# Moving the sums and low parts of one fp32 network kernel from GpSimd to VectorE, each placed apart

## The chip, the cores and the metric

One core of one Trainium2 chip runs the whole program. The metric is the device time of one execution in microseconds (us), lower is better. Engines are named as in the profile: PE is TensorE (matrix products), PEld its weight load, DVE is VectorE, ACT is ScalarE, POOL is GpSimd, SP is SyncE, whose queue issues the DMAs.

## The reference

A channel attention over 6016 tokens and 256 channels, followed by two feed-forward networks with 2048 hidden channels, all in fp32:

```python
qn = q / (np.linalg.norm(q, axis=1, keepdims=True) + 1e-06)
kn = k / (np.linalg.norm(k, axis=1, keepdims=True) + 1e-06)
s = kn.transpose(0, 2, 1) @ qn / tau
a = softmax(s)                       # rows of a 256 x 256 matrix
x = v @ a                            # 6016 x 256
h = x @ moe_w_in
x = (h * np.clip(h + 3.0, 0.0, 6.0) / 6.0) @ moe_w_out
r = np.maximum(x @ moe2_w_in, 0.0)
return (r * r) @ moe2_w_out
```

## The kernel before

**Arithmetic.** Every fp32 operand of a product is kept as two tiles of a rounded type (fp32r): a high part, which ScalarE makes by a cast, and a low part, the value less its high part, which is one subtraction. `passes` then issues three matmuls for one product (lines 308, 309 and 310: high by high, low by high, high by low). The attention matrix is multiplied into the first network's input weights, so the kernel computes two feed-forward networks one after the other (`j` = 0 and 1).

**Tiling.** The tokens lie in six pairs of blocks (`p` = 0 to 5), each block 512 tokens wide and 448 in the last pair. The hidden channels lie in eight units (`u`) of 256. For each pair and unit `strassen` multiplies a 2 x 2 block of weights by a 2 x 2 block of tokens with seven products in place of eight; the pair (0, 0) alone goes the plain way. One unit is 21 matmuls for the seven products and 24 that multiply the activated hidden values by the output weights (`group`): 45 matmuls. There are eleven Strassen pairs, so 88 units.

**What the seven products need.** For tokens: the sums T1 to T4 of the four blocks, and seven high and seven low parts, made by `prepare` for the next pair while the current one runs (`combination`: line 708, low parts: line 715; 11 subtractions a pair). For weights: four sums (`combine`, line 214) and their low parts, made by `m1_sum` and `m1_sums_split` for the first network's four blocks `c4`, and by `second_in` (sums, line 214; `rests`, line 244) and `second_out` (line 123) for each of eight parts of the second network, which are written to DRAM and read back when the second network begins. All of these subtractions and sums run on GpSimd: 16 instructions of `m1_sum`, 8 of `m1_sums_split`, 121 of `prepare`, 48 of `second_in` and 8 of `second_out`, 201 in all. The raw weights come as float64 and are turned into fp32 by two ScalarE and four VectorE instructions (`from_float64`, lines 152 to 165).

**What VectorE does in a unit.** Eleven instructions of the unit's width: three sums that finish a hidden block (line 761; one operand comes from PSUM), four activations (line 775 in the first network, 780 in the second; where the hidden block is `h` both operands lie in SBUF, where it is `y` one lies in PSUM) and four low parts of the activated blocks (line 123, `gs<-g,gs`, both operands in SBUF).

**The order.** It is written out by hand: `at(place, go)` puts a step at a place, and `run` issues the steps of all engines by rising place. A unit is 15 places (`SLOTS`), one place for each group of three matmuls, and a unit's steps have fixed places after its start (`PLACE`, `chain`, `GROUP`). Each engine then runs its own steps in that order, as early as its operands allow. The place numbers below count from the first Strassen unit; the eight units of pair p of the first network begin at 120 (p - 1), those of the second at 600 + 120 p. GpSimd's steps go through `on_pool`, which moves a step later by 0.3 until it stands at least `POOL_APART` = 3.2 places from every other step so placed.

Of the kernel before, what the change touches and what calls it, by code (L numbers as in the profile page):

```python
# [41 lines left out]
POOL_APART = 3.2  # L42
# [11 lines left out]
def attention_then_two_ffns(  # L54
# [63 lines left out]
    def split(hi, lo, x, part=2, rest=None):  # L118

        if part != 1:  # L120
            nc.scalar.copy(hi, x)  # L121
        if part != 0:
            (rest or nc.vector).tensor_tensor(out=lo, in0=x, in1=f32(hi), op=ALU.subtract)  # L123
# [83 lines left out]
    def combine(i, st, a, b):  # L207
# [6 lines left out]
        nc.gpsimd.tensor_tensor(out=b(st, to), in0=x, in1=y, op=op)  # L214

    def second_in(u):
# [25 lines left out]
        def rests(i):  # L242
            a, w = ((slice(0, S1), x[:, :S1, :]), (slice(S1, None), st))[i]
            nc.gpsimd.tensor_tensor(out=lo[:, a, :], in0=w, in1=f32(hi[:, a, :]), op=ALU.subtract)
# [7 lines left out]
    def second_out(u):  # L252
# [6 lines left out]
        def parts(x, part):  # L259
# [3 lines left out]
            split(t[:, 0, :], t[:, 1, :], x, part, rest=nc.gpsimd)  # L263
# [48 lines left out]
    with tc.manual_schedule():  # L312
# [166 lines left out]
        def m1_keep(c4):  # L479
            for k in range(KC):  # L480
                if k == 0:
                    m32[c4] = spare(2 * c4 + 1, f"m32_{c4}").rearrange("p (k f) -> p k f", k=KC)
# [195 lines left out]
        def prepare(j, p, start, end):  # L678
# [15 lines left out]
            def combination(r):  # L694
# [13 lines left out]
                nc.gpsimd.tensor_tensor(out=to, in0=x, in1=y, op=ALU.subtract)  # L708
# [10 lines left out]
            for i, r in enumerate((T1, T2)):  # L719
                on_pool(start + 12 + 4 * i, lambda r=r: combination(r))  # L720
            for r, x in when.items():
                at(start + x, lambda r=r: hi(r))
                on_pool(start + x + 1.7, lambda r=r: lo(r))
            for i, r in enumerate((T3, T4)):
                on_pool(start + 32 + 4 * i, lambda r=r: combination(r))

            first_pair = {T3: 0.3, T1: -14.5, B22: 4.3, T4: -10.5}
            for i, r in enumerate((T3, T1, B22, T4)):
                after = first_pair[r] if (j, p) == (0, 1) else end - SLOTS + 8.3 + 4 * i
                at(after, lambda r=r: hi(r))  # L730
                on_pool(after + 1.7, lambda r=r: lo(r))
# [222 lines left out]
```

## Time and profile before

| | us |
|---|---|
| runs of before | 1064.50, 1062.21, 1064.21; median 1064.21 |
| profiled execution, whole | 1063.71 |
| its span, first to last instruction | 1061.9 |
| TensorE busy | 1042.6 |
| VectorE busy | 864.2 |
| ScalarE busy | 664.6 |
| GpSimd busy | 251.4 |

Busy times are the time in which an engine had an instruction under way. Matmuls overlap each other, so that TensorE can count as busy and still run below its pace: what tells its pace is how many matmuls it starts in a stretch of time. A row of the timeline gives the start, the duration, the engine, the source line, the operation and its tiles; in square brackets it gives how long the engine stood idle before and what ended that.

### The profile page before, as it was taken

To read this page: it belongs to the slowest core of one execution; us is meant where nothing else is said; L and a number is where in the kernel's file an instruction comes from. 1 tells how busy PE (TensorE), PEld (TensorE's weight loads), DVE (VectorE), ACT (ScalarE), POOL (GpSimd) and SP (SyncE) were. 2 spreads that over 40 slices of the span, in tenths; PEclk is the share of its full clock that TensorE was granted. 3 is DMA by queue.
4 is the path that set the end of the run, shared out by engine and by line. 5 is a ranking of instruction groups with operands and counts; after the bars stand their busy time and mean duration, and the time that the engine had idled before them with its cause. 6 is when DMAs were issued, how large, how long until landed. Compare 5 with 4: busy or idle time off the path is not lost.

```text
span 1061.9 us, 13045 instructions
## 1 busy us (share of the span) xinstructions
PE 1042.6 (98%) x4630; PEld 865.0 (81%) x4630; DVE 864.2 (81%) x1283; ACT 664.6 (63%) x1200; POOL 251.4 (24%) x211
## 2 busy tenths in 40 slices
PE   9999999999999999999999999999999999999998
PEld 8867777887877888787998888888888888888997
DVE  7898867898898889888889678678778878778766
ACT  6777767777777778776777445455445445545443
POOL 0012244343134133324233022113103104103000
PEclk9999999999999999999999999999999999999999
DMA  9911203102302301320765100100200200200100
GB/s 352 349 42 40 80 1 120 55 20 95 119 0 102 137 31 40 115 90 0 243 236 211 49 1 36 44 1 6 74 1 1 80 1 0 75 1 1 40 1 35
DMA packets 25938, 77.65 MB, mean 73 GB/s; under 512 B 2833, under 2 KB 4881, under 8 KB 25873
## 3 DMA queue, kind: packets, MB, share of 16 engines
q1 hardware_dynamic: 25872, 76.82, 20.4%
q8 instruction: 36, 0.59, 0.2%
q14 instruction: 30, 0.24, 0.1%
HBM read 52.95 MB, written 23.86 MB: 72 GB/s over the span
## 4 chain that ended last, share of the span: by engine, by line
PE 78%; DVE 14%; ACT 6%; issue 2%; POOL 0%; ACTq 0%; POOLq 0%
PE acc L310 13%; PE acc L308 13%; PE acc L309 13%; PE y L308 6%; PE y L309 6%; PE y L310 6%; DVE gs L123 4%; PE s L298 4%; PE q L308 3%; PE q L309 3%; PE q L310 3%; DVE g L775 3%; PE x L308 2%; PE x L310 2%; PE x L309 2%
## 5 line engine op out<-in xcount | busy, mean ns | idle before, releaser
L123 DVE TENSOR_TENSOR gs<-g,gs 128x512 fp32r<-128x512 f32 (+1 forms) x384 | 293.2, 764 | 71.3 <-ACT gs L784 61.7
L310 PE MATMUL acc<-gs,wo 128*128 128x512 f32 (+1 forms) x768 | 298.2, 388 | 5.1 <-DVE gs L123 5.0
L308 PE MATMUL acc<-gs,wo 128*128 128x512 f32 (+1 forms) x768 | 296.6, 386 | 1.6 <-ACT gs L121 1.0
L309 PE MATMUL acc<-gs,wo 128*128 128x512 f32 (+1 forms) x768 | 296.0, 385 | 0.0
L784 ACT CAST gs<-g 128x512 fp32r<-128x512 f32 (+1 forms) x352 | 208.5, 614 | 79.5 <-DVE g L775 55.9
L310 PEld LDWEIGHTS acc<-gs,wo 128*128 128x128 f32 x768 | 144.1, 188 | 39.9 <-DVE gs L123 12.9
L308 PEld LDWEIGHTS acc<-gs,wo 128*128 128x128 f32 x768 | 144.3, 188 | 29.9 <-ACT gs L121 2.2
L309 PEld LDWEIGHTS acc<-gs,wo 128*128 128x128 f32 x768 | 144.3, 188 | 26.7
L715 POOL TENSOR_TENSOR x<-raw,x 128x512 fp32r<-128x512 f32 (+1 forms) x55 | 73.1, 1330 | 368.6 <-ACT x L711 367.1
L780 DVE SCALAR_TENSOR_TENSOR g<-h 128x512 f32<-128x512 f32 (+1 forms) x144 | 120.5, 837 | 0.0
L761 DVE TENSOR_TENSOR h<-q,se 128x512 f32<-128x512 f32 (+1 forms) x88 | 59.5, 676 | 64.3 <-ACT se L757 64.3
L757 ACT COPY se<-y 128x512 f32<-128x512 f32 (+1 forms) x88 | 50.6, 575 | 92.5 <-PE y L310 92.2
L775 DVE SCALAR_TENSOR_TENSOR g<-r,h 128x512 f32<-128x512 f32 (+1 forms) x120 | 104.5, 871 | 3.5 <-ACT r L767 2.9
L757 ACT COPY su<-y 128x512 f32<-128x512 f32 (+1 forms) x88 | 50.8, 577 | 87.4 <-PE y L310 77.1
L767 ACT ACTIVATE r<-h,three 128x512 f32<-128x512 f32 (+1 forms) x120 | 85.6, 714 | 12.5 <-DVE h L761 12.2
L769 ACT ACTIVATE r<-y 128x512 f32<-128x512 f32 (+1 forms) x48 | 28.3, 590 | 56.7 <-PE y L310 56.6
L761 DVE TENSOR_TENSOR h<-q,su 128x512 f32<-128x512 f32 (+1 forms) x88 | 59.2, 673 | 1.0
L761 DVE TENSOR_TENSOR h<-x,sa 128x512 f32<-128x512 f32 (+1 forms) x88 | 59.1, 672 | 0.0
L757 ACT COPY sa<-y 128x512 f32<-128x512 f32 (+1 forms) x88 | 50.7, 576 | 7.0 <-PE y L310 0.9
L780 DVE SCALAR_TENSOR_TENSOR g<-y,r 128x512 f32<-128x512 f32 (+1 forms) x48 | 32.5, 677 | 19.9 <-ACT r L769 19.6
L298 PE MATMUL s<-qk 128*128 128x256 f32 x188 | 42.8, 389 | 0.0
L298 PEld LDWEIGHTS s<-qk 128*128 128x128 f32 x188 | 36.4, 196 | 5.5 <-DMA qk<-in_qk 0.6
(234 smaller groups left out, 1856.8 us busy)
## 6 DMA issues: line engine op xcount, KB each, us to landing
qk<-in_qk SPq DMA_DIRECT2D x23, 512.0 KB, 7.4
wo<-in_w_out SPq DMA_DIRECT2D x16, 512.0 KB, 5.8
wi<-in_w_in SPq DMA_DIRECT2D x10, 512.0 KB, 4.9
x2d<-o SPq DMA_DIRECT2D x20, 256.0 KB, 2.6
raw<-x2d SPq DMA_DIRECT2D x10, 512.0 KB, 5.8
out<-o SPq DMA_DIRECT2D x20, 256.0 KB, 2.3
raw<-in_vt SPq DMA_DIRECT2D x8, 512.0 KB, 6.4
wo2d<-wo2s SPq DMA_DIRECT2D x8, 512.0 KB, 3.0
```

Source lines behind the costliest of these rows:

```text
L123: (rest or nc.vector).tensor_tensor(out=lo, in0=x, in1=f32(hi), op=ALU.subtract)
L298: nc.tensor.matmul(s_ps[i], lhsT=x[:, C + i * P:C + (i + 1) * P], rhs=x[:, :C], start=(t == 0), stop=(t == NT - 1))
L308: nc.tensor.matmul(ps, lhsT=ah, rhs=bh, start=first, stop=False, skip_group_check=more)
L309: nc.tensor.matmul(ps, lhsT=al, rhs=bh, start=False, stop=False, skip_group_check=more)
L310: nc.tensor.matmul(ps, lhsT=ah, rhs=bl, start=False, stop=last, skip_group_check=more)
L715: nc.gpsimd.tensor_tensor(out=l, in0=ts[r], in1=f32(h), op=ALU.subtract)
L757: nc.scalar.copy(s[tag], s["y"])
L761: nc.vector.tensor_tensor(out=s[which], in0=s[ps], in1=s[tag], op=ALU.add)
L767: nc.scalar.activation(s["r" + which], h, AF.Relu, bias=three)
L775: nc.vector.scalar_tensor_tensor(out=g, in0=s["r" + which], scalar=6.0, in1=h, op0=ALU.min, op1=ALU.mult)
L780: nc.vector.scalar_tensor_tensor(out=g, in0=h, scalar=0.0, in1=r, op0=ALU.max, op1=ALU.mult)
L784: nc.scalar.copy(gs[which][0], s["g" + which])
```

## The change

From the second Strassen pair on, all of GpSimd's sums and low parts are issued on VectorE. GpSimd keeps those of the pair (0, 1), 11 instructions, and of the weight blocks c4 = 0 and 1, 12 instructions; the other 178 move. `on_pool` becomes `extra`: every step that goes through it now stands at least `APART` = 2.6 places from every other (3.2, as before, for places up to 0). The VectorE steps of `from_float64` for the second network's weights go through `extra` too, one by one (`converted`), where before they stood at fixed places. The sums of the weight blocks c4 = 2 and 3 begin at places 10 and 34 (before -9 and 17), and the second network's weights are prepared from unit 3.5 on, one part each 4.05 units (before from unit 2, each 4.5).

```diff
-POOL_APART = 3.2
+APART = 2.6
+APART_FIRST = 3.2
...
-    def combine(i, st, a, b):
+    def combine(i, st, a, b, eng=nc.vector):
...
-        nc.gpsimd.tensor_tensor(out=b(st, to), in0=x, in1=y, op=op)
+        eng.tensor_tensor(out=b(st, to), in0=x, in1=y, op=op)
...
-            nc.gpsimd.tensor_tensor(out=lo[:, a, :], in0=w, in1=f32(hi[:, a, :]), op=ALU.subtract)
+            nc.vector.tensor_tensor(out=lo[:, a, :], in0=w, in1=f32(hi[:, a, :]), op=ALU.subtract)
...
-            split(t[:, 0, :], t[:, 1, :], x, part, rest=nc.gpsimd)
+            split(t[:, 0, :], t[:, 1, :], x, part)
...
+        def idle_first(first):
+
+            return nc.gpsimd if first else nc.vector
...
-            split(hi, lo, m1_st[c4][:, u, :, :], part, rest=nc.gpsimd)
+            split(hi, lo, m1_st[c4][:, u, :, :], part, idle_first(c4 < 2))
...
-        def on_pool(place, go):
-
-            while any(abs(place - x) < POOL_APART for x in taken):
+        def extra(place, go):
+
+
+            while any(abs(place - x) < (APART if place > 0 else APART_FIRST) for x in taken):
                 place += 0.3
             taken.append(place)
             at(place, go)
...
-                nc.gpsimd.tensor_tensor(out=to, in0=x, in1=y, op=ALU.subtract)
+                idle_first((j, p) == (0, 1)).tensor_tensor(out=to, in0=x, in1=y, op=ALU.subtract)
...
-                nc.gpsimd.tensor_tensor(out=l, in0=ts[r], in1=f32(h), op=ALU.subtract)
+                idle_first((j, p) == (0, 1)).tensor_tensor(out=l, in0=ts[r], in1=f32(h), op=ALU.subtract)
...
-        for c4, x in enumerate((-100, -72, -9, 17)):
+        for c4, x in ((0, -100), (1, -72), (2, 10), (3, 34)):
             for i in range(4):
-                x = on_pool(x, lambda c4=c4, i=i: m1_sum(c4, i)) + 1
+                x = extra(x, lambda c4=c4, i=i: m1_sum(c4, i)) + 1
             for u in range(2):
-                at(x + 3 + u, lambda c4=c4, u=u: m1_sums_split(c4, u, 0))
+                at(x + 2 + u, lambda c4=c4, u=u: m1_sums_split(c4, u, 0))
             for u in range(2):
-                x = on_pool(x + 5 - 4 * u, lambda c4=c4, u=u: m1_sums_split(c4, u, 1))
+                x = extra(x + 4 - 3 * u, lambda c4=c4, u=u: m1_sums_split(c4, u, 1))
...
+        def converted(begin, make):
+
+            made = []
+            at(begin, lambda: made.extend(make()))
+            at(begin + 8.7, lambda: made[0][0]())
+            x = begin + 8.7
+            for i in range(1, 4):
+                x = extra(x + (1.6, 1.6, 1.3)[i - 1], lambda i=i: made[0][i]())
+            return made, x
+
         def prepare_in(u, begin):
-            made = []
-            at(begin, lambda: made.extend(second_in(u)))
-            for i, x in enumerate((8.7, 9.5, 17.3, 19.4, 22.4)):
-                at(begin + x, lambda i=i: made[0][i]())
-            x = begin + 22.4
+            made, x = converted(begin, lambda: second_in(u))
+            at(x + 1.6, lambda: made[0][4]())
+            x += 4
             for i in range(4):
-                x = on_pool(x + 3, lambda i=i: made[1](i))
-            at(x + 4, lambda: made[2]())
+                x = extra(x, lambda i=i: made[1](i)) + 0.7
+            at(x + 1, lambda: made[2]())
+            x += 3.5
             for i in range(2):
-                x = on_pool(x + 6 - 2 * i, lambda i=i: made[3](i))
-            at(x + 6, lambda: made[4]())
+                x = extra(x, lambda i=i: made[3](i))
+            at(x + 4, lambda: made[4]())
...
         for u in range(NU):
-            prepare_in(u, (2 + 4.5 * u) * SLOTS)
-            prepare_out(u, (4.25 + 4.5 * u) * SLOTS)
+            prepare_in(u, (3.5 + 4.05 * u) * SLOTS)
+            prepare_out(u, (5.5 + 4.05 * u) * SLOTS)
```

`prepare_out` is rewritten in the same way with `converted` and `extra`. The line numbers of the changed file are higher by one near `combine` and by ten in `prepare` and `strassen`.

What this makes of VectorE's order is seen at the start of pair (0, 3). `g`, `h` and `gs` are a unit's activated blocks, hidden blocks and their parts, `o` an output block that leaves PSUM, `tawi`/`tawo` the conversion of the second network's weights, `wa2s` the low parts of its weights, `x` and `raw` the tokens of the next pair, and the two numbers after a name are pair and unit. Before:

```order
L775 SCALAR_TENSOR_TENSOR g_3_0_3173<-r_3_0_3164,h_3_0_3137 128x512
L160 SCALAR_TENSOR_TENSOR tawi_3_3109<-tbwi_3_3110,tawi_3_3109 128x512
L581 TENSOR_SCALAR o_2_1_0_3179<-acc_2_1_0_2446 128x512
L165 ISA tawi_3_3109<-tawi_3_3109,tywi_3_3111 128x1024
L761 TENSOR_TENSOR h_3_0_3197<-q_3_0_3159,se_3_0_3186 128x512
L123 TENSOR_TENSOR gs_3_0_3192<-g_3_0_3173,gs_3_0_3192 128x512
L581 TENSOR_SCALAR o_2_0_1_3211<-acc_2_0_1_2428 128x512
L775 SCALAR_TENSOR_TENSOR g_3_0_3222<-r_3_0_3206,h_3_0_3197 128x512
L775 SCALAR_TENSOR_TENSOR g_3_0_3233<-r_3_0_3224,y_3_0_3098 128x512
L761 TENSOR_TENSOR h_3_0_3239<-q_3_0_3159,su_3_0_3155 128x512
```

The same stretch of VectorE's order now:

```order
L725 TENSOR_TENSOR x_3_6_3141<-raw_3_1_2750,x_3_6_3141 128x512
L124 TENSOR_TENSOR gs_2_7_3150<-g_2_7_3143,gs_2_7_3150 128x512
L785 SCALAR_TENSOR_TENSOR g_3_0_3166<-r_3_0_3157,h_3_0_3130 128x512
L245 TENSOR_TENSOR wa2s_3034<-w_2_2771,wa2s_3033 128x384
L590 TENSOR_SCALAR o_2_1_0_3172<-acc_2_1_0_2423 128x512
L245 TENSOR_TENSOR wa2s_3034<-w_2_2771,wa2s_3033 128x512
L771 TENSOR_TENSOR h_3_0_3189<-q_3_0_3152,se_3_0_3178 128x512
L124 TENSOR_TENSOR gs_3_0_3183<-g_3_0_3166,gs_3_0_3183 128x512
L590 TENSOR_SCALAR o_2_0_1_3203<-acc_2_0_1_2411 128x512
L785 SCALAR_TENSOR_TENSOR g_3_0_3210<-r_3_0_3198,h_3_0_3189 128x512
L161 SCALAR_TENSOR_TENSOR tawo_2_2915<-tbwo_2_2916,tawo_2_2915 128x512
L785 SCALAR_TENSOR_TENSOR g_3_0_3224<-r_3_0_3213,y_3_0_3094 128x512
```

The low parts of the pair's own tokens and of the second network's weights now stand between the unit's steps, and the two conversion steps (lines 160 and 165) ahead of `h` have gone to other places.

GpSimd's order at the same place of the program, before:

```order
L715 TENSOR_TENSOR x_3_3_3058<-raw_3_0_2753,x_3_3_3058 128x512
L715 TENSOR_TENSOR x_3_4_3084<-t_3_0_2830,x_3_4_3084 128x512
L715 TENSOR_TENSOR x_3_5_3115<-raw_3_1_2754,x_3_5_3115 128x512
L715 TENSOR_TENSOR x_3_6_3148<-raw_3_1_2754,x_3_6_3148 128x512
L244 TENSOR_TENSOR wa2s_3065<-w_2_2750,wa2s_3064 128x384
L244 TENSOR_TENSOR wa2s_3065<-w_2_2750,wa2s_3064 128x512
L123 TENSOR_TENSOR wo2s_2975<-tawo_2_2877,wo2s_2975 128x512
L214 TENSOR_TENSOR w_3_3215<-w_3_3215 128x128 x4
```

GpSimd's order now ends with the pair (0, 1), the one that the first Strassen units multiply:

```order
L718 TENSOR_TENSOR raw_1_1_1169<-raw_1_1_1169,t_1_1_1248 128x512
L725 TENSOR_TENSOR x_1_4_1436<-t_1_0_1247,x_1_4_1436 128x512
L725 TENSOR_TENSOR x_1_6_1459<-raw_1_1_1169,x_1_6_1459 128x512
L725 TENSOR_TENSOR x_1_3_1497<-raw_1_0_1168,x_1_3_1497 128x512
L725 TENSOR_TENSOR x_1_5_1516<-raw_1_1_1169,x_1_5_1516 128x512
L962 UNCONDITIONAL_BRANCH
```

Nothing of pair (0, 3) or of the second network's weights is left on GpSimd.

## Rows read from the trace of the kernel before

**Rows 1.** The page's head and busy times: us, share of the span, instructions.
```profile
span 1061.9 us, 13045 instructions
...
PE 1042.6 (98%) x4630; PEld 865.0 (81%) x4630; DVE 864.2 (81%) x1283; ACT 664.6 (63%) x1200; POOL 251.4 (24%) x211
```
**Rows 2.** Busy by stretch: pairs (0,2) to (0,5), (1,1), six units of (1,5).
```profile
core 0: us, PE busy (x) PEld busy (x) DVE busy (x) ACT busy (x) POOL busy (x), PEclk, DMA share, GB/s
...
237.82:324.14 86.32, 82.91 (x361) 67.12 (x360) 74.29 (x106) 64.26 (x114) 25.08 (x23) 1.00 0.19 66
324.14:410.34 86.20, 83.57 (x361) 68.38 (x360) 74.97 (x106) 63.49 (x113) 28.04 (x24) 0.98 0.23 83
410.34:494.96 84.62, 83.49 (x361) 67.05 (x360) 72.36 (x103) 62.99 (x114) 28.48 (x26) 1.00 0.22 77
494.96:570.56 75.60, 74.84 (x361) 67.08 (x360) 67.75 (x103) 57.58 (x111) 27.11 (x24) 1.00 0.56 195
651.60:733.24 81.64, 81.64 (x362) 67.58 (x361) 63.31 (x91) 40.66 (x73) 15.61 (x12) 1.00 0.09 26
...
987.96:1042.68 54.72, 54.72 (x272) 50.72 (x271) 38.12 (x68) 24.19 (x48) 0.00 (x0) 1.00 0.04 16
```
**Rows 3.** Waits of TensorE: us in total, times, longest us.
```profile
PE acc L310 <- DVE gs L123: 5.0, 8, 1.8
PE q L308 <- DVE h L761: 3.6, 2, 2.6
```
**Rows 4.** Timeline of VectorE ahead of TensorE's longest wait: start, us.
```profile
329.69 1.77 DVE L775 SCALAR_TENSOR_TENSOR g<-r,h 128x512 f32<-128x512 f32 x1
...
332.81 1.77 DVE L775 SCALAR_TENSOR_TENSOR g<-r,h 128x512 f32<-128x512 f32 x1
334.51 1.77 DVE L160 SCALAR_TENSOR_TENSOR tawi<-tbwi,tawi 128x512 int32<-128x512 int32 x1
...
336.80 0.67 DVE L165 CUSTOM_DVE_ANT_0 tawi<-tawi,tywi 128x1024 uint16<-128x1024 uint16 x1
337.40 0.68 DVE L761 TENSOR_TENSOR h<-q,se 128x512 f32<-128x512 f32 x1
```
**Rows 5.** Timeline of GpSimd in the same stretch.
```profile
330.88 3.16 POOL L244 TENSOR_TENSOR wa2s<-w,wa2s 128x384 fp32r<-128x384 f32 x2
334.00 1.73 POOL L123 TENSOR_TENSOR wo2s<-tawo,wo2s 128x512 fp32r<-128x512 f32 x1
```
**Rows 6.** Timeline of TensorE: the matmul that waited for it.
```profile
338.13 0.79 PE L308 MATMUL q<-x,wa_0h 128*128 128x512 f32 x1 [2.63 <-DVE h L761]
```
**Rows 7.** Groups of VectorE by line and shape: busy us, mean ns | idle before.
```profile
L123 DVE TENSOR_TENSOR gs<-g,gs 128x512 fp32r<-128x512 f32 x320 | 249.1, 778 | 60.3 <-ACT gs L784 51.1 <-ACT gs L121 6.7
L780 DVE SCALAR_TENSOR_TENSOR g<-h 128x512 f32<-128x512 f32 x120 | 105.6, 880 | 0.0
L775 DVE SCALAR_TENSOR_TENSOR g<-r,h 128x512 f32<-128x512 f32 x96 | 83.3, 868 | 2.9 <-ACT r L767 2.3
...
L761 DVE TENSOR_TENSOR h<-x,sa 128x512 f32<-128x512 f32 x72 | 49.3, 684 | 0.0
...
L775 DVE SCALAR_TENSOR_TENSOR g<-r,h 128x448 f32<-128x448 f32 x24 | 21.2, 883 | 0.6 <-ACT r L767 0.6
...
L160 DVE SCALAR_TENSOR_TENSOR tawi<-tbwi,tawi 128x512 int32<-128x512 int32 x16 | 13.7, 855 | 0.1
...
L407 DVE TENSOR_SCALAR scratch<-both,scratch 128x128 f32<-128x128 f32 x2 | 0.5, 286 | 0.0
```
**Rows 8.** Group of ScalarE: the cast ahead of a token block's low part.
```profile
L711 ACT CAST x<-raw 128x512 fp32r<-128x512 f32 x45 | 27.8, 618 | 1.1 <-PE q L310 1.1
```
**Rows 9.** Timelines of VectorE and GpSimd where the tokens of pair (1,0) land.
```profile
545.42 0.62 DVE L761 TENSOR_TENSOR h<-x,sa 128x448 f32<-128x448 f32 x1
...
545.75 1.29 POOL L708 TENSOR_TENSOR t<-raw 128x512 f32<-128x512 f32 x1 [7.05 <-DMA raw<-x2d]
```
**Rows 10.** Waits of VectorE: us in total, times, longest us.
```profile
DVE h L761 <- ACT se L757: 64.3, 57, 1.9
```

More of the change, by code (lines that the diff above doesn't have):

```diff
@@ L116, in f32, with split @@
         return x.bitcast(F32)
-    def split(hi, lo, x, part=2, rest=None):
+    def split(hi, lo, x, part=2, eng=nc.vector):
         if part != 1:
@@ L122, in split @@
         if part != 0:
-            (rest or nc.vector).tensor_tensor(out=lo, in0=x, in1=f32(hi), op=ALU.subtract)
+            eng.tensor_tensor(out=lo, in0=x, in1=f32(hi), op=ALU.subtract)
     def wa_tiles(c4, name):
@@ L481, in m1_keep, with beside @@
                 if k == 0:
-                    m32[c4] = spare(2 * c4 + 1, f"m32_{c4}").rearrange("p (k f) -> p k f", k=KC)
+                    m32[c4] = beside(c4, 1).rearrange("p (k f) -> p k f", k=KC)
                 nc.scalar.activation(m32[c4][:, k, :], mps.pop((c4, k)), AF.Copy, scale=rsum[k])
         m1_st = {}
+        def idle_first(first):
+            return nc.gpsimd if first else nc.vector
+        def beside(c4, i):
+            return spare(2 * c4 + i, f"m32_{c4}{i}")
         def m1_sum(c4, i):
             if i == 0:
-                m1_st[c4] = spare(2 * c4, f"st{c4}").rearrange("p (u a c) -> p u a c", u=2, a=4)
+                m1_st[c4] = beside(c4, 0).rearrange("p (u a c) -> p u a c", u=2, a=4)
             m = [m32[c4][:, k, :].rearrange("p (u f c) -> p u f c", u=2, f=2) for k in range(KC)]
-            combine(i, m1_st[c4], [[t[:, :, f, :] for f in range(2)] for t in m], lambda t, i: t[:, :, i, :])
+            combine(i, m1_st[c4], [[t[:, :, f, :] for f in range(2)] for t in m], lambda t, i: t[:, :, i, :], idle_first(c4 < 2))
         def m1_sums_split(c4, u, part):
             hi, lo = (t[:, u, S1:, :] for t in wa1[c4])
-            split(hi, lo, m1_st[c4][:, u, :, :], part, rest=nc.gpsimd)
+            split(hi, lo, m1_st[c4][:, u, :, :], part, idle_first(c4 < 2))
         def m1_part(c4, i):
@@ L719, in prepare @@
             for i, r in enumerate((T1, T2)):
-                on_pool(start + 12 + 4 * i, lambda r=r: combination(r))
+                extra(start + 12 + 4 * i, lambda r=r: combination(r))
             for r, x in when.items():
                 at(start + x, lambda r=r: hi(r))
-                on_pool(start + x + 1.7, lambda r=r: lo(r))
+                extra(start + x + 1.7, lambda r=r: lo(r))
             for i, r in enumerate((T3, T4)):
-                on_pool(start + 32 + 4 * i, lambda r=r: combination(r))
+                extra(start + 32 + 4 * i, lambda r=r: combination(r))
             first_pair = {T3: 0.3, T1: -14.5, B22: 4.3, T4: -10.5}
@@ L730, in prepare @@
                 at(after, lambda r=r: hi(r))
-                on_pool(after + 1.7, lambda r=r: lo(r))
+                extra(after + 1.7, lambda r=r: lo(r))
         def strassen(j, p, u, at0):
@@ L848, in load_wo2 @@
             nc.sync.dma_start(out=f32(wo_of[u]), in_=wo2_d[u])
[L850 to L855 removed]
+        def converted(begin, make):
[6 more added lines that the diff above has]
+            return made, x
+        def prepare_in(u, begin):
+            made, x = converted(begin, lambda: second_in(u))
+            at(x + 1.6, lambda: made[0][4]())
+            x += 4
             for i in range(4):
[L857 to L858 removed]
+                x = extra(x, lambda i=i: made[1](i)) + 0.7
+            at(x + 1, lambda: made[2]())
+            x += 3.5
             for i in range(2):
[L860 to L861 removed]
+                x = extra(x, lambda i=i: made[3](i))
+            at(x + 4, lambda: made[4]())
         def prepare_out(u, begin):
[L864 to L870 removed]
+            made, x = converted(begin, lambda: second_out(u))
+            at(x + 1.6, lambda: made[0][4](0))
+            x = extra(x + 3, lambda: made[0][4](1))
+            at(x + 4, lambda: made[1]())
         for u in range(NU):
[L873 to L874 removed]
+            prepare_in(u, (3.5 + 4.05 * u) * SLOTS)
+            prepare_out(u, (5.5 + 4.05 * u) * SLOTS)
         last = unit_at[1, 0]
```

7 lines of the change are left out of this document (removed).

## The prediction

> **What bounds the kernel now.** I read the busy times first: TensorE has a matmul under way in 98% of the span, VectorE is busy for 81% [rows 1]. That says TensorE bounds, but matmuls overlap, so the share does not tell whether TensorE runs at its pace. For that I cut the span at the first matmul of each pair and compared stretches that hold the same work. Pair (1,1) takes 81.64 us with no idle time [rows 2], which is 10.20 us a unit and 0.227 us a matmul (81.64 / 360). Pairs (0,2), (0,3) and (0,4) issue as many matmuls and take 86.32, 86.20 and 84.62 us [rows 2]. They lose 4.7, 4.6 and 3.0 us. Pair (0,5) is narrower: six such units take 54.72 us in the last pair [rows 2], 9.12 us each, so eight take 73.0; its first unit still has 24 accumulations of 512 columns, worth 24 x (0.227 - 0.203) = 0.6. Its 75.60 us [rows 2] holds a loss of 2.0. Together **14.3 us are lost in pairs (0,2) to (0,5)**, and nothing in the second network. That is all that this change can win there.
>
> The waits of TensorE tell who is late: VectorE, with a low part (5.0 us) and a hidden sum (3.6 us) [rows 3]. The rest is short ScalarE waits, gaps too short to be listed, and about 1.7 us in pair (0,3), where the granted clock averages 0.98 [rows 2].
>
> Why is VectorE late? Ahead of the longest wait, two activations and a conversion step take 1.77 us each, and only then come the steps in front of `h` [rows 4]. GpSimd is busy without a gap from 330.88 to 335.73 beside them [rows 5], and TensorE stands for 2.63 us until `h` is there [rows 6]. The groups show the same over the whole run: a VectorE instruction with one operand in PSUM takes 684 ns (`h<-x,sa`), but those with both in SBUF average 778, 880 and 868 ns [rows 7]. Such an instruction is held while GpSimd works, for up to 1.77 - 0.68 = 1.09 us.
>
> **The change part by part.** *What goes.* The holding. Over 684 ns [rows 7]: 320 x 0.094 + 120 x 0.196 + 96 x 0.184 = 71 us; the 448-wide activations, over 0.60 us (684 ns x 7/8), 24 x 0.28 = 7; the 16 steps of line 160 shown, 16 x 0.17 = 3, and some 10 us for the groups of the same kinds that are not shown. I take 90 us, about 80 of it behind the first pair, where GpSimd falls silent.
>
> *What comes.* 178 instructions on VectorE. One that follows another directly starts 0.60 us after it, though each lasts 0.67 to 0.69 (336.80 to 337.40) [rows 4]. So: 108 of 512 columns at 0.60 = 65; 22 of 448 at 0.53 = 12; 8 of 384 at about 0.47 and 8 of 256 at 0.34 = 6; 32 of 128, which no row shows for this operation, between 0.13 (a quarter of the columns' share, 0.53 / 4) and 0.29 (the 128-column form) [rows 7], taken at 0.20 = 6. Sum 89 us (87 to 92). **VectorE's total stays where it is, about 860 us**, but it comes in pieces of 0.6 us, put at chosen places, in place of surprises of 1.1 us.
>
> *Is there room?* The thickest part is from unit 3.5 to 36. A unit needs 11 x 0.60 = 6.6 us of VectorE. A part of the second network's weights, every 4.05 units, needs two conversions of 2 x 0.34 + 2 x 0.60 = 1.9, four sums of 0.2, and 0.47 + 0.60 + 0.60 of low parts: 6.2, or 1.54 a unit (0.34 is half the columns' share and 0.07 to start). A token pair adds 11 x 0.60 / 8 = 0.83, two output copies a pair 0.15. Sum 9.1 of 10.2 us, 89%. At the start of a pair the order stacks conversions and output copies; counted from the order, the two units there need 10.1 to 10.4 us. Here no margin is left.
>
> *Who is late next.* In places 0.2 to 5.4 of a unit seven of the eleven steps stand: 4.2 us of work in 3.5. By this queue alone the low part of block 22, at place 2.8, starts 0.7 us late. Its matmul, the third pass of the group at place 6, is 3.9 places or 2.6 us behind it; less 0.75 for the step itself, 1.9 us of delay are free. Before, two holdings (2.2 us) overdraw that. Now at most two added steps stand ahead of it (2.6 places apart), 0.7 + 1.2 = 1.9: just met. Hence single added steps cost nothing; they are hidden by those 1.9 us, and where ScalarE is late as well, TensorE stops.
>
> *New waits.* A low part waits for ScalarE's cast, 1.7 places (1.16 us) ahead of it; the cast takes 0.62 [rows 8], so 0.5 us is spare. When the cast is later, everything behind it on VectorE waits too, and TensorE behind that. GpSimd's waiting held nobody up. I allow 1 us of loss in each of the three crowded pair starts and nothing elsewhere: 3 us. The bounds are 0 and, worked out below, 25 or more.
>
> *Queues and edges.* On SP the stores of weights and the token loads stand in a slightly other order; each store still waits for a step that VectorE does at its place. The tokens of pair (1,0) land at 545.75, when VectorE is at the `h` that starts at 545.42 and comes next to the sum that reads them [rows 9]: 0 to 0.5 us, inside the 1.9. In the second network the pair's 11 added steps meet VectorE at 63.31 of 81.64 us [rows 2], with 12 GpSimd instructions gone: no loss. The first 166 us keep GpSimd's work, so 0 within 0.5 us. The clock's dip in pair (0,3) should go with the 2.63 us stop in front of it; it is in the 14.3.
>
> *Sum.* 1063.7 - 14.3 + 3.0 = 1052.4 for the profiled execution, whose span [rows 1] has 1.8 us around it; the median of the runs is 0.5 above it. I predict **1052.6**.
>
> **The rivals.** *A. VectorE fills up.* If a step costs its whole 0.685 us and not 0.60, the 9.1 us a unit become 10.4, 0.2 over the unit; over 32.5 units 6.5 us come back on top of the 3: 1059.1. The pitch [rows 4] speaks against it. The Trainium skill's page "VectorE: DVE Perf Modes", section "The DRAIN you can't avoid", says that a next instruction does not start until the pipe of the one before is empty; it adds that one which is not held starts earlier. By the first sentence rival A would be the forecast; by the second, and by the trace's 0.60 us between starts, it is not.
>
> *B. The casts come late (slower than before).* 0.88 token low parts and 0.74 weight steps a unit wait for ScalarE. VectorE has 1.1 us a unit to spare, so a mean wait above 0.68 us uses it up (1.1 / 1.62). At 1.13 us, the mean of VectorE's present wait for `se` (64.3 us in 57 waits) [rows 10], a unit takes 1.62 x 1.13 - 1.1 = 0.73 us longer; 32.5 units cost 24, so 1063.7 - 14.3 + 24 = 1073. It decides from a mean of 1.0 us, where the 14.3 and 2 more are eaten. Against it: the spare 0.5 us, and that ScalarE is itself late today mostly because it waits for a VectorE that is held.
>
> *C. Half the gain.* The stacked pair starts overdraw the 1.9 us every time, by 2 us in each of four pairs: 1063.7 - 14.3 + 8 = 1057.4.
>
> *D. It doesn't do what it says.* The same losses come back from queueing in place of holding, 14 us: 1063.5. For it: the seven steps in 3.5 us leave no slack today. Against it: those steps with up to two holdings a pair in the second network lose nothing at all [rows 2].
>
> **How the numbers follow.** Forecast 0.57, C 0.17, A 0.08 give faster 0.82; D 0.07 gives the same; B 0.11 gives slower. About 0.2%, 2.1 us, is what a measurement of this kernel can tell from no change. The range reaches from the forecast with nothing left of the loss (1049.5) over C and A to 1061; B and D, 0.18, are left out.
>
> **What would show it.** Pairs (0,2) to (0,4) at 81.6 to 83 us each; low parts `gs` at 0.69 us on average; GpSimd busy for under 35 us; VectorE in total within 10 us of 864; TensorE's waits for VectorE under 3 us after 166 us. Wrong would be the forecast if VectorE is idle, waiting for line 721's casts, for more than 0.5 us each, or if the units at the start of a pair are 1 us longer than the others. That VectorE is held by GpSimd would be wrong if the 1.77 us instructions stay after GpSimd's work is gone.

## The result, and the profile after

The changed kernel takes **1049.71 us** (median of four runs, 1049.39 to 1051.51); the kernel before, run beside it, takes 1064.36 (1062.21 to 1065.04). The ratio is **0.986, 95% interval 0.9846 to 0.9874**: 14.6 us are gone. Forecast were 1052.6 and a range from 1049.5, so the time lies at the range's low end; by the ratio, the 1064.21 shown before would become 1049.3, just under it. The profiled execution went from 1063.71 to 1050.01, its span by 13.7.

First the page's head and busy times of after, to be held against [rows 1]:

```profile
span 1048.2 us, 12985 instructions
...
PE 1035.9 (99%) x4630; PEld 865.5 (83%) x4630; DVE 863.7 (82%) x1461; ACT 665.7 (64%) x1200; POOL 29.7 (3%) x33
```

VectorE has 178 instructions more and is busy for 0.5 us less. Now the stretches of after by pair, (0,2) to (0,5) and (1,1), with the columns of [rows 2]:

```profile
237.69:319.29 81.60, 81.60 (x362) 67.59 (x361) 75.18 (x132) 65.01 (x115) 0.00 (x0) 1.00 0.25 88
319.29:400.89 81.60, 81.60 (x362) 67.59 (x360) 74.48 (x130) 64.43 (x114) 0.00 (x0) 1.00 0.25 87
400.89:482.92 82.03, 81.99 (x362) 67.44 (x360) 74.45 (x131) 64.05 (x113) 0.00 (x0) 1.00 0.24 85
482.92:556.94 74.02, 73.98 (x362) 67.48 (x360) 67.19 (x124) 57.83 (x110) 0.00 (x0) 1.00 0.56 192
...
637.97:719.57 81.60, 81.60 (x362) 67.60 (x361) 63.67 (x103) 40.40 (x73) 0.00 (x0) 1.00 0.09 27
```

The pairs that took 86.32, 86.20, 84.62 and 75.60 us [rows 2] now take 81.60, 81.60, 82.03 and 74.02: 13.5 us. Pair (0,1) gives another 0.40 (its last seven units take 71.42 after 71.82), and its first unit, the first Strassen unit of all, begins 0.27 later: 13.6 of the 13.7. The 0.27 tell nothing: in the kernels below, most of which share that beginning, this unit starts anywhere from 157.9 to 160.4 us. Two pairs run at exactly the length of pair (1,1), which has little else to do on VectorE. The granted clock of pair (0,3) is 1.00, after 0.98. What is left over is one unit of pair (0,4) (10.63 us where its neighbours take 10.20) and one of pair (0,5) (9.43 against 9.12).

TensorE's waits for VectorE, after, over the whole run (us, times, longest):

```profile
PE acc L311 <- DVE gs L124: 1.4, 2, 1.2
```

Of the 8.6 us of [rows 3] these 1.4 are left, both waits ahead of 166 us (at 70 and 125 us), where GpSimd keeps its work. VectorE's groups, after, answering to [rows 7]:

```profile
L124 DVE TENSOR_TENSOR gs<-g,gs 128x512 fp32r<-128x512 f32 x320 | 221.1, 691 | 47.1 <-ACT gs L794 37.5 <-ACT gs L122 6.7
L790 DVE SCALAR_TENSOR_TENSOR g<-h 128x512 f32<-128x512 f32 x120 | 82.1, 684 | 0.0
L785 DVE SCALAR_TENSOR_TENSOR g<-r,h 128x512 f32<-128x512 f32 x96 | 65.9, 686 | 3.4 <-ACT r L777 3.4
...
L771 DVE TENSOR_TENSOR h<-x,sa 128x512 f32<-128x512 f32 x72 | 49.2, 683 | 0.0
...
L725 DVE TENSOR_TENSOR x<-raw,x 128x512 fp32r<-128x512 f32 x40 | 27.4, 685 | 0.0
...
L215 DVE TENSOR_TENSOR w<-w 128x128 f32<-128x128 f32 x32 | 9.1, 284 | 0.0
```

778, 880 and 868 ns became 691, 684 and 686: nothing is held any more. The moved low parts of tokens (line 725) last 685 ns, and none of their idle time is put down to a cast.

### The profile page after: what moved, and what is told of

It reads as the page before. It is cut to its first block, busy times and chain, and to the rows that moved or that the text cites. A ratio compares the mean times of both kernels' runs of the same rounds, so it can differ in the third digit from the quotient of the medians.

```text
span 1048.2 us, 12985 instructions
## 1 busy us (share of the span) xinstructions
PE 1035.9 (99%) x4630; PEld 865.5 (83%) x4630; DVE 863.7 (82%) x1461; ACT 665.7 (64%) x1200; POOL 29.7 (3%) x33
## 4 chain that ended last, share of the span: by engine, by line
PE 86%; DVE 6%; ACT 3%; DMA 2%; issue 1%; SPq 0%; ACTq 0%; DVEq 0%
PE acc L311 15%; PE acc L309 15%; PE acc L310 15%; PE y L309 7%; PE y L311 7%; PE y L310 7%; PE q L309 4%; PE q L311 4%; PE q L310 4%; PE x L309 2%; PE x L311 2%; PE x L310 2%; DMA qk<-in_qk 2%; DVE gs L124 1%; DVE g L631 1%
## 5 line engine op out<-in xcount | busy, mean ns | idle before, releaser
L124 DVE TENSOR_TENSOR gs<-g,gs 128x512 fp32r<-128x512 f32 (+1 forms) x384 | 260.6, 679 | 55.8 <-ACT gs L794 46.0
L790 DVE SCALAR_TENSOR_TENSOR g<-h 128x512 f32<-128x512 f32 (+1 forms) x144 | 97.0, 673 | 0.0
L785 DVE SCALAR_TENSOR_TENSOR g<-r,h 128x512 f32<-128x512 f32 (+1 forms) x120 | 80.8, 673 | 3.8 <-ACT r L777 3.8
L296 DVE TENSOR_TENSOR scratch<-sq,scratch 128x512 f32<-128x512 f32 x47 | 29.3, 684 | 8.1 <-ACT sq L295 8.1
```

The source lines that it names most:

```text
L124: eng.tensor_tensor(out=lo, in0=x, in1=f32(hi), op=ALU.subtract)
L296: nc.vector.tensor_tensor(out=sums[t % 2], in0=sq, in1=sums[t % 2], op=ALU.add)
L785: nc.vector.scalar_tensor_tensor(out=g, in0=s["r" + which], scalar=6.0, in1=h, op0=ALU.min, op1=ALU.mult)
L790: nc.vector.scalar_tensor_tensor(out=g, in0=h, scalar=0.0, in1=r, op0=ALU.max, op1=ALU.mult)
```

## The experiments

Each edit is made to the changed kernel unless another is named; line numbers shift by a few. A ratio is to the kernel before, run on the same chip beside it.

### Is it the engine or the places?

The change does two things: the work leaves GpSimd, and every extra step, the conversions of the second network's weights among them, gets a place of its own. Two kernels do one each. The first keeps the new places, and gives the 178 steps back to GpSimd:

```diff
-    def combine(i, st, a, b, eng=nc.vector):
+    def combine(i, st, a, b, eng=nc.gpsimd):
...
-                idle_first((j, p) == (0, 1)).tensor_tensor(out=to, in0=x, in1=y, op=ALU.subtract)
+                nc.gpsimd.tensor_tensor(out=to, in0=x, in1=y, op=ALU.subtract)
```

> The changed kernel's places, but all 201 sums and low parts stay on GpSimd. Theory (VectorE was late because GpSimd holds its two-SBUF-operand instructions): the holding is back, low parts gs at 0.75 us or more on average, 1058 to 1066 us. Rival (the gain comes from the new places, the conversions apart and the later weights): near 1050 us.

Measured: 1054.86 us, ratio 0.9904 [0.9888, 0.9921]. Both expectations missed: the time lies between them. Its busy line, and its groups of VectorE:

```profile
PE 1039.3 (99%) x4630; PEld 864.1 (82%) x4630; DVE 851.9 (81%) x1283; ACT 665.4 (63%) x1200; POOL 253.4 (24%) x211
...
L124 DVE TENSOR_TENSOR gs<-g,gs 128x512 fp32r<-128x512 f32 x320 | 244.1, 763 | 62.1 <-ACT gs L794 52.4 <-ACT gs L122 6.7
L790 DVE SCALAR_TENSOR_TENSOR g<-h 128x512 f32<-128x512 f32 x120 | 105.6, 880 | 0.0
L785 DVE SCALAR_TENSOR_TENSOR g<-r,h 128x512 f32<-128x512 f32 x96 | 88.5, 922 | 5.6 <-ACT r L777 5.5
```

VectorE's activations are held as much as before (880 and 922 ns), and still 10 us are won. Of the 5 us above the changed kernel, 0.9 are the narrower pair's last five units, which run at 9.30 us here and at 9.12 there; more on them below.

The second kernel is the kernel before with the same steps on VectorE at their old places (GpSimd keeps the first pair's and c4 = 0 and 1):

```diff
-            nc.gpsimd.tensor_tensor(out=lo[:, a, :], in0=w, in1=f32(hi[:, a, :]), op=ALU.subtract)
+            nc.vector.tensor_tensor(out=lo[:, a, :], in0=w, in1=f32(hi[:, a, :]), op=ALU.subtract)
...
```

> The kernel before with its old places; the same 178 instructions go to VectorE as in the change. Theory (holding): gs at 0.68 us, most of the 14 us back, 1050 to 1056 us, what is above 1050 being the price of the old places on a VectorE that has more to do. Rival (places): 1062 us or more.

Measured: 1053.11 us, ratio 0.9886 [0.9871, 0.9901], inside the range of the theory. Pairs (0,2) to (0,5) take 81.60, 83.81, 81.87 and 73.76 us; one unit of pair (0,3) (12.38 us) makes 2.2 of the 2.5 us that are left there and in (0,4). VectorE in that unit (start, duration):

```profile
329.75 0.69 DVE L165 CUSTOM_DVE_ANT_0 tawi<-tawi,tywi 128x1024 uint16<-128x1024 uint16 x1
...
331.56 0.69 DVE L581 TENSOR_SCALAR o<-acc 128x512 f32<-128x512 f32 x1
332.15 0.69 DVE L244 TENSOR_TENSOR wa2s<-w,wa2s 128x512 fp32r<-128x512 f32 x1
...
334.21 0.69 DVE L775 SCALAR_TENSOR_TENSOR g<-r,y 128x512 f32<-128x512 f32 x1 [0.77 <-ACT r L767]
...
335.42 0.68 DVE L123 TENSOR_TENSOR wo2s<-tawo,wo2s 128x512 fp32r<-128x512 f32 x1
336.01 0.69 DVE L123 TENSOR_TENSOR gs<-g,gs 128x512 fp32r<-128x512 f32 x1
```

and TensorE, waiting for that last step:

```profile
336.75 0.50 PE L310 MATMUL acc<-gs,wo 128*128 128x512 f32 x1 [0.63 <-DVE gs L123]
```

A conversion, an output copy and two low parts of weights stand close together, 0.6 us each, ahead of the low part that TensorE needs; and VectorE itself waits 0.77 us there for an activation of ScalarE, which is late as well.

The third kernel is the first one (GpSimd, new places, later starts) with the whole preparation of the second network's weights back at its old offsets: the conversions at fixed places, no longer kept apart from GpSimd's steps, and GpSimd's steps on these weights at their old distances behind them. Of this edit, the conversions' part:

```diff
-                x = extra(x + (1.6, 1.6, 1.3)[i - 1], lambda i=i: made[0][i]())
...
+            for i, x in enumerate((8.7, 9.5, 17.3, 19.4, 22.4)):
+                at(begin + x, lambda i=i: made[0][i]())
```

> All sums and low parts on GpSimd, at the changed places and starts, but the conversions' steps at their old fixed offsets, not apart (compare e1_places_only, 1054.9 us, which has them apart). If before lost its time where a conversion step stands right in front of a step that TensorE needs and both are held, the loss comes back: 1060 to 1066 us. If what helped in e1_places_only was the later start and the wider pitch of GpSimd's own steps: 1054 to 1056 us.

Measured: 1066.97 us, ratio 1.0014 [1.0003, 1.0024], just above the range of the first expectation: all that the first kernel won is gone. So its gain comes from the places inside this preparation, and not from the later starts or the changed spacing of GpSimd's other steps. That it is the conversions, and not GpSimd's steps behind them, is argued and not shown by itself, as the edit moves both; what speaks for it are their durations. Two things happen to a conversion at a place of its own. Steps no longer stand in a row, and GpSimd is not at work beside it: with the old offsets VectorE's busy time is 862.0 us, with the new ones 851.9. One of the conversion's groups, first of the third kernel, then of the first:

```profile
L158 DVE TENSOR_SCALAR tbwo<-tbwo 128x512 f32<-128x512 f32 x16 | 9.9, 618 | 0.0
```
```profile
L158 DVE TENSOR_SCALAR tbwo<-tbwo 128x512 f32<-128x512 f32 x16 | 6.7, 421 | 0.0
```

In the third kernel three of these sixteen steps have GpSimd at work beside them and last 1.38 to 1.52 us, the others 0.41 to 0.43. So this step is held too, though it reads one operand only. The four combinations are:

| | weights prepared at old offsets | at new places, each step apart |
|---|---|---|
| steps on GpSimd | 1064.4 (before), 1066.97 (later starts) | 1054.86 |
| steps on VectorE | 1053.11 | 1049.71 (after) |

Either cure alone wins 10 to 12 us, both together 14.7. The two do not add.

### Does the spacing matter for the moved steps?

```diff
-APART = 2.6
+APART = 0.01
```

> The changed kernel with a spacing of 0.01 places in place of 2.6: the added steps and the conversions stand where they first fall, up to seven in a row. If a late step costs TensorE time only beyond some 2 us of VectorE's delay (the prediction's 1.9), a row of five to seven added steps, 3 to 4 us, overdraws it once or twice for each of the eight weight parts: 8 to 15 us, 1057 to 1065 us. Rival (the engine alone matters, the spacing is idle): 1050 to 1052 us.

Measured: 1056.56 us, ratio 0.9913 [0.9895, 0.9932], just under what was expected. VectorE's durations are those of after (691 ns for the low parts), its total is 863.9, and yet the last seven units of pair (0,1) take 72.97 us, and the pairs (0,2) to (0,5) 84.38, 82.94, 82.3 and 74.11. The same work, stacked, costs 6.0 us more in these stretches (6.8 by the medians).

### Is the holding real, and what is it worth alone?

The changed kernel, with work on GpSimd that nobody waits for: after each of the 70 moved low parts of tokens GpSimd subtracts the same operands in four quarters into a dummy tile.

```diff
+                if (j, p) != (0, 1):
+                    for q in range(4):
+                        a = slice(q * w // 4, (q + 1) * w // 4)
+                        nc.gpsimd.tensor_tensor(out=dum[:, :w // 4], in0=ts[r][:, a], in1=f32(h)[:, a], op=ALU.subtract)
```

> The changed kernel; GpSimd repeats the token pairs' low parts from (0,2) on into a tile that nobody reads, in four quarters, right after the cast. Nothing on VectorE waits for it. Theory (holding): VectorE's two-SBUF instructions beside it take up to 1.7 us again, and as VectorE is at 89% in the first network the time rises by 5 to 25 us, to 1055 to 1075. Rival (places): no more than 1 us, 1050 to 1051.

Measured: 1054.90 us, ratio 0.9908 [0.989, 0.9925], just under what the theory gave and well above the rival's 1051. The twin of it reads one column only and then fills the dummy tile eight times, so that GpSimd writes and hardly reads:

```diff
+                if (j, p) != (0, 1):
+                    nc.gpsimd.tensor_tensor(out=dum[:, :1], in0=ts[r][:, :1], in1=f32(h)[:, :1], op=ALU.subtract)
+                    for _ in range(8):
+                        nc.gpsimd.memset(dum, 0.0)
```

> As the shadow, but GpSimd reads one column and then fills the tile eight times, 1.6 us of writing without reading, after each of the 70 casts. If any activity of GpSimd holds VectorE: as the shadow, 1055 to 1075. If only its reads of SBUF do: gs at 0.68 us, 1050 to 1051.

Measured: 1051.54 us, ratio 0.9871 [0.9856, 0.9886], half a microsecond above what was expected if only reads hold. The busy line and groups of VectorE, first with GpSimd's reads:

```profile
PE 1038.7 (99%) x4630; PEld 864.4 (82%) x4630; DVE 898.5 (85%) x1461; ACT 669.9 (64%) x1200; POOL 221.7 (21%) x314
...
L126 DVE TENSOR_TENSOR gs<-g,gs 128x512 fp32r<-128x512 f32 x320 | 229.2, 716 | 42.9 <-ACT gs L800 34.4 <-ACT gs L124 6.7
L796 DVE SCALAR_TENSOR_TENSOR g<-h 128x512 f32<-128x512 f32 x120 | 89.9, 749 | 0.0
...
L727 DVE TENSOR_TENSOR x<-raw,x 128x512 fp32r<-128x512 f32 x40 | 36.6, 916 | 0.0
```

then with its fills:

```profile
PE 1036.5 (99%) x4630; PEld 864.8 (82%) x4630; DVE 863.8 (82%) x1461; ACT 665.6 (63%) x1200; POOL 172.7 (16%) x664
...
L126 DVE TENSOR_TENSOR gs<-g,gs 128x512 fp32r<-128x512 f32 x320 | 221.3, 692 | 47.1 <-ACT gs L800 37.5 <-ACT gs L124 6.7
L796 DVE SCALAR_TENSOR_TENSOR g<-h 128x512 f32<-128x512 f32 x120 | 82.3, 686 | 0.0
```

With the fills GpSimd is busy for 143 us more than in after, but VectorE's durations don't move (692 and 686 ns). With the reads VectorE is busy for 35 us more than in after, and 5 us of that reach the end. So VectorE is held by what GpSimd reads, and not by its being busy. The Trainium skill says so, on the page "SBUF — State Buffer", section "Who interferes with whom": a VectorE instruction with two SBUF inputs contends with a GpSimd instruction that reads SBUF, not with one that only writes it. These two kernels agree. Of the fills' 1.8 us over after, 1.0 lies in pair (0,5) (75.02 us), whose last five units take 9.30 us and not 9.12 at a granted clock of 1.00; that appears in the kernel with the new places alone and in the one without work on GpSimd (below), too, and is not explained. In the profiled execution the rest lies ahead of the first Strassen unit.

### Which of the moved steps count?

Two kernels move one half each: the tokens' steps alone (68 of weights back on GpSimd), and the weights' alone (110 of tokens back).

```diff
-            nc.vector.tensor_tensor(out=lo[:, a, :], in0=w, in1=f32(hi[:, a, :]), op=ALU.subtract)
+            nc.gpsimd.tensor_tensor(out=lo[:, a, :], in0=w, in1=f32(hi[:, a, :]), op=ALU.subtract)
...
```

> The changed places; only the token pairs' sums and low parts are on VectorE, the 80 steps of the weights stay on GpSimd. Between e1_places_only (1054.9 us, all on GpSimd) and the changed kernel (1050). By holding: GpSimd's time in the first network is cut by more than half, so most of the 4.7 us goes: 1050.5 to 1052.5 us, with gs at 0.70 us and the second network free of holding.

Measured: 1049.72 us, ratio 0.9844 [0.9829, 0.9858], better than expected. The unit of pair (0,4) that after leaves at 10.63 us takes 10.20 here, and the pairs take 81.60, 81.62, 81.60 and 74.06.

```diff
-                idle_first((j, p) == (0, 1)).tensor_tensor(out=l, in0=ts[r], in1=f32(h), op=ALU.subtract)
+                nc.gpsimd.tensor_tensor(out=l, in0=ts[r], in1=f32(h), op=ALU.subtract)
...
```

> The reverse of e5_tokens_only: the sums and low parts of the weights are on VectorE, the token pairs' 121 steps stay on GpSimd, all at the changed places. e5 came out at 1049.7 us although GpSimd still worked for 95 us, so by subtraction the 4.7 us that e1_places_only keeps above the changed kernel belong to the token steps: 1053 to 1056 us, lost in the second and third unit of the pairs (0,2) to (0,4). If instead the two halves only cost together, as engine and places do: 1050 to 1051.5 us.

Measured: 1054.82 us, ratio 0.9893 [0.9871, 0.9915], as expected, and the time of the kernel with all 178 on GpSimd. The tokens' steps alone are the engine's part of the gain; at the new places, where the weights' steps run makes no difference that these runs can tell. The remaining one has no GpSimd work for tokens and weights at all, the first pair's included:

```diff
-            return nc.gpsimd if first else nc.vector
+            return nc.vector
```

> The changed kernel with the last 23 instructions off GpSimd too (pair (0,1) and the weight blocks c4 = 0 and 1). In the stretch from 60 to 160 us VectorE is already busy for some nine tenths of the time, so by the room theory 23 more steps, some 12 us in 100, cost 2 to 6 us: 1052 to 1056 us. If being held is what costs there as well: 1046 to 1049 us.

Measured: 1050.95 us, ratio 0.986 [0.9843, 0.9877], the same as after; neither expectation held. GpSimd is busy for 1.2 us in all. Ahead of 166 us TensorE's waits for the low parts fall from 1.4 to 0.2 us, but most of its other gaps stay, and the first Strassen unit begins only 0.4 us earlier; pair (0,5), with its last five units at 9.30 us, gives 0.9 back.

### How much delay is free?

The prediction rests on 1.9 us of free delay for the low part of block 22. In the second network the units are quiet and all alike, so a known delay can be put at a unit's head: 5, 7, 9 or 12 dummy subtractions on VectorE, one number for each of four pairs, each step on the result of the one before.

```diff
+            def late(n):
+                for _ in range(n):
+                    nc.vector.tensor_tensor(out=dum, in0=dum, in1=dum, op=ALU.subtract)
+
+            if j == 1 and 1 <= p <= 4 and u >= 2:
+                at(at0 + 0.1, lambda: late((5, 7, 9, 12)[p - 1]))
```

> The changed kernel; in the second network, in units 2 to 7 of the pairs (1,1) to (1,4), a row of 5, 7, 9 and 12 short VectorE steps (128 columns, some 0.2 us each, about 1.0, 1.4, 1.8 and 2.4 us) stands at the unit's start, ahead of block 22. It measures VectorE's free delay, which the prediction put at 1.9 us with 0.7 us of it used. If that is right: nothing lost with 5, up to 0.2 us a unit with 7, some 0.6 with 9, 1.2 with 12, 12 us in all, 1060 to 1063 us. If the free delay is larger by half a microsecond or more, as the changed kernel's pair starts suggest: nothing with 5 and 7, under 0.2 with 9, 0.7 with 12, 1052 to 1056 us.

Measured: 1070.08 us, ratio 1.004 [1.0024, 1.0056]; neither expectation held. A dummy in such a chain costs more than was planned; a row of VectorE's timeline gives 3.88 us for twelve, 0.325 each:

```profile
943.96 3.88 DVE L803 TENSOR_TENSOR dum<-dum 128x128 f32<-128x128 f32 x12
```

One unit of each pair, without steps for tokens (columns as in [rows 2]):

```profile
668.00:678.20 10.20, 10.20 (x46) 8.45 (x45) 8.16 (x16) 4.67 (x8) 0.00 (x0) 1.00 0.01 2
749.82:760.02 10.20, 10.20 (x47) 8.45 (x45) 8.74 (x18) 4.67 (x8) 0.00 (x0) 1.00 0.00 0
833.79:844.30 10.51, 10.50 (x46) 8.37 (x45) 9.33 (x20) 4.72 (x8) 0.00 (x0) 1.00 0.00 0
921.60:933.10 11.50, 10.78 (x46) 8.29 (x45) 10.21 (x23) 4.71 (x8) 0.00 (x0) 1.00 0.01 1
```

1.6 and 2.3 us of delay cost nothing, 2.9 cost 0.31 and 3.9 cost 1.30: the last microsecond costs one. Measured at the low part of block 22 itself, as its start less the time at which TensorE passes its place, the four are 0.77, 1.42, 2.07 and 3.06 us late; less the losses, both of the last two give a limit of **1.76 us**. Most of the 20 us lost are lost in the units with token steps, where the dummies and the low parts add up: the seventh units of (1,2) and (1,3) are 3.22 and 4.22 us late and lose 1.46 and 2.47, which is again the lateness less 1.76. One unit of this kernel breaks the rule, the seventh of (1,4): 4.93 late, 5.97 lost. There TensorE waits for a cast of ScalarE as well. In the changed kernel that low part is 1.32 us late in the second unit of pairs (0,2) and (0,3), which lose nothing, and 2.12 in the unit of 10.63 us, 0.36 over the limit, with 0.43 lost. There, VectorE's row of that low part, in the changed kernel's timeline:

```profile
425.38 0.69 DVE L124 TENSOR_TENSOR gs<-g,gs 128x512 fp32r<-128x512 f32 x1
```

and TensorE's at the same place, whose last matmul needs it:

```profile
425.46 0.39 PE L309 MATMUL acc<-gs,wo 128*128 128x512 f32 x1
425.69 0.39 PE L310 MATMUL acc<-gs,wo 128*128 128x512 f32 x1
426.12 0.50 PE L311 MATMUL acc<-gs,wo 128*128 128x512 f32 x1
```

It starts 0.43 us after the one ahead of it, where 0.23 is the pace, just behind the low part's end at 426.07. This stop of 0.2 us is in no list of waits, and the rest of the 0.43 is spread over smaller ones.

### The rivals of the prediction

Rival A, a full VectorE: every moved low part of weights (`rests`) and tokens is done twice, 86 instructions more.

```diff
-            nc.vector.tensor_tensor(out=lo[:, a, :], in0=w, in1=f32(hi[:, a, :]), op=ALU.subtract)
+            for _ in range(2):
+                nc.vector.tensor_tensor(out=lo[:, a, :], in0=w, in1=f32(hi[:, a, :]), op=ALU.subtract)
...
```

> The changed kernel with 86 of the moved low parts (those of the token pairs and of the input weights) done twice in a row on VectorE. At 0.60 us a step the first network's load rises from 9.1 to 9.9 of 10.2 us a unit, the pair starts to about 11: no overall overload, 1 to 2 us lost at each of four pair starts, 1054 to 1060 us. If a step costs its whole 0.685 us (rival A of the prediction), the load is 11.3 us a unit and the time rises by 30 us or more, to 1080.

Measured: 1063.54 us, ratio 0.9987 [0.9975, 0.9998]: above the first expectation and far under the second. The twins are dearer than was planned. A twin writes the tile that the step before it writes, and it starts 0.72 us after that step; the steps behind the two start 0.60 us apart, as in [rows 4]:

```profile
322.31 1.41 DVE L727 TENSOR_TENSOR x<-raw,x 128x512 fp32r<-128x512 f32 x2
323.64 0.68 DVE L773 TENSOR_TENSOR h<-q,se 128x512 f32<-128x512 f32 x1
324.24 0.68 DVE L124 TENSOR_TENSOR gs<-g,gs 128x512 fp32r<-128x512 f32 x1
```

And only 51 of the 86 twins, 35 of tokens and 16 of weights, fall into the first network: some 35 us, where the 32.5 units had 1.1 us spare each, 36 in all. By rival A, where a unit is overfilled without them, all 35 us had to come on top; 13.8 did. So A falls here, and with the pitch of 0.60 us in the rows, and with the changed kernel itself, whose units run at 10.20 us where A wanted 10.4. The 13.8 us are lost for the most part in single units. The largest losses are in the second units of the pairs (0,2) to (0,4), some 2.3 us each: their low part of block 22 is 2.1 to 2.2 us late, which accounts for 0.3 to 0.4, and for 1.6 us TensorE waits for another step, the hidden sum `h`, which reads the PSUM tile `q` before TensorE adds to it again. So that low part is not the only step with a deadline. TensorE's longest waits here:

```profile
PE q L310 <- DVE h L773: 5.7, 5, 1.6
PE acc L312 <- DVE gs L124: 3.1, 6, 1.4
```

Rival B, late casts: each low part of tokens is placed 0.2 places behind its cast, where the change has 1.7.

```diff
-                extra(start + x + 1.7, lambda r=r: lo(r))
+                extra(start + x + 0.2, lambda r=r: lo(r))
...
-                extra(after + 1.7, lambda r=r: lo(r))
+                extra(after + (1.7 if (j, p) == (0, 1) else 0.2), lambda r=r: lo(r))
```

> The changed kernel with each low part of a token block placed 0.2 in place of 1.7 places behind its cast, so that VectorE reaches it half a microsecond or more before ScalarE is done and waits, with all that is queued behind it. Rival B of the prediction made such waits decisive: at 0.5 us for each of 70 low parts, 35 of them in the first network, some 5 to 10 us at the pair starts, 1055 to 1060 us. If the free delay covers a single wait: 1050 to 1052 us, with waits of line 725 for line 721 in the profile and no more of TensorE.

Measured: 1058.09 us, ratio 0.9924 [0.991, 0.9939], inside the range expected for rival B. VectorE's wait for the cast, and TensorE's for VectorE:

```profile
DVE x L725 <- ACT x L721: 28.8, 34, 1.9
```
```profile
PE acc L311 <- DVE gs L124: 4.9, 10, 0.7
```

34 waits of 0.85 us bring 8 us back. They are lost where the low part of block 22 misses its deadline. The first two units of pair (0,2), columns as in [rows 2]:

```profile
238.39:249.58 11.19, 10.52 (x46) 8.37 (x45) 10.06 (x18) 9.61 (x17) 0.00 (x0) 1.00 0.02 7
249.58:260.47 10.89, 10.50 (x46) 8.37 (x45) 10.38 (x19) 7.70 (x14) 0.00 (x0) 1.00 0.77 271
```

In them that low part is 2.72 and 2.44 us late, 0.96 and 0.68 over the 1.76, and they lose 0.99 and 0.69. The mechanism is real; the 1.5 places between cast and low part keep it out of the change, where this wait is not among VectorE's.

## Why the prediction was right or wrong

**What can be won.** Right within 0.6 us: 14.3 us counted, of which the pairs (0,2) to (0,5) gave 13.5 and still hold 0.8. That nothing is won elsewhere was off by 0.40 in pair (0,1), whose length it had not compared, and by 0.27 the other way at the first unit's start, which varies by more than that.

**VectorE's total.** Right: about 860 us forecast, 863.7 measured; low parts at 691 ns, GpSimd at 29.7 us, TensorE's waits for VectorE behind 166 us under 3.

**The holding.** Right that it goes and that GpSimd causes it; reads do, fills don't. But the prediction named it as the one cause of VectorE's lateness, and it is one of two. With the activations held as before, the new places won 10 us, in part because the conversions no longer stand beside GpSimd's work; with the conversions left stacked, ending the holding won 12. That places count without any holding shows in the kernel without spacing, which is held nowhere behind the first pair and loses 6 us. Both stand in its rows, the held steps and the conversion steps in front of the longest wait [rows 4], but the new places got no term. Its sum did not suffer, since it added up lost time and not causes. For the engine alone the same reasoning came out right (1050 to 1056 expected, 1053.11 measured), for the new places alone it came out wrong (1058 to 1066 expected, 1054.86 measured).

**The free delay.** Right for the low part of block 22: 1.9 us worked out, 1.76 measured. The hidden sum `h`, for which TensorE waited longest before [rows 6], got no such number, and none was measured.

**The allowance of 3 us: the step that failed.** "I allow 1 us of loss in each of the three crowded pair starts and nothing elsewhere" was the term of the sum that was mis-sized: 0.8 us were left in pairs (0,2) to (0,5), 0.43 and 0.31 of it in two units. The first two units of pairs (0,2) and (0,3), counted at 10.1 to 10.4 of 10.2 us, lost nothing. A unit at its brim does not lose a microsecond; it runs a little later, into the 1.76 us that are free, and the next, emptier units bring it back: in the first five units of pair (0,2) the low part of block 22 is 0.63, 1.32, 1.05, 0.55 and 0.28 us late. The term had to be the lateness of the step whose deadline comes first, here that low part, less the free delay: 1.32 - 1.76, nothing, and 2.12 - 1.76 = 0.4. The 0.31 are of a unit of 448 columns, for which no limit was measured. With 0.8 for 3.0, and the 0.40 and 0.27, the sum would have been 1050.1 for the profiled execution, which took 1050.01. So the allowance makes 2.2 of the 2.9 us by which the forecast was too high. The rest is small: the 0.40 less the 0.27, and the step from the profiled execution to the median, which the sum names as 0.5 up and adds as 0.2 (1052.4 to 1052.6), and which was 0.3 down (1050.01 to 1049.71). The bottom of the range was "nothing left of the loss" in four pairs, and so had no room for the fifth.

**The rivals.** A falls with the 0.60 us between steps, with units of 10.20 us and with the doubled steps. B has its mechanism, and needs the cast nearer than 1.7 places; its price does not hold. By its sum waits of 0.85 us on 0.88 token steps a unit use up 0.75 of the 1.1 us that VectorE has to spare, and nothing is lost; 8 us were, since the deadline of one step is missed long before the spare time of a unit is gone. C and D are out by the pairs' lengths; but D is what the kernel without spacing does in part (6 us come back from queueing).

**What stays open.** Why the narrower pair's last five units take 9.30 us in some kernels and 9.12 in others, 0.9 us in all. What delay is free at the hidden sum `h`. And whether the kernel with the weights' steps on GpSimd, 1049.72 us, is better than after, 1049.71: their ratios were taken beside different runs of before, and overlap. No version is faster than the change by more than the noise.

## What to carry to other kernels

Work that moves from GpSimd to VectorE can be free even where VectorE looks nearly full: what it adds (89 us by count) may be no more than the holding that goes with GpSimd's reads, and VectorE's total tells (864.2 and 863.7 us). Ask of each added step not how full its stretch is, but how late the steps that TensorE waits for become, and take off the delay that is free at each; here one such step, the low part of block 22, was enough for the changed kernel, and not for the kernels with doubled steps or with GpSimd's reads, where `h` cost more. Two causes that overdraw the same free delay together must not be priced one by one: taking away either won 10 or 12 us of 14.7.

## What the runs showed of the hardware

VectorE was held by GpSimd's reads alone: 143 us of fills left its low parts at 692 ns, reads in the same places brought three of its groups to 716, 749 and 916. A one-operand conversion step took up to 1.52 us beside GpSimd's work and 0.42 elsewhere. Independent VectorE steps of 512 columns start 0.60 us apart while each lasts 0.68, and a step of 128 columns is followed after 0.20 us. Dependent ones overlap less: a step that writes the tile the one before it writes starts 0.72 us after it (512 columns), and in a chain, where each step needs the one before, 128 columns took 0.325 us a step. And a delay of VectorE shows a sharp edge on TensorE in this kernel: at the low part of block 22 nothing up to 1.76 us and, where no other step was late, one for one beyond (2.07 us late: 0.31 lost; 4.22 late: 2.47 lost).
